# Attention and two mixture layers on one core: token pairs of 256, 512 and 320 columns in place of 256, 384 and 448

## The chip, the cores and the metric

The program runs on one core of one Trainium2 chip. The metric is the device time of one execution in microseconds (us); lower is better. The engines are named as in the profile: PE is TensorE (PEld its weight loads), DVE is VectorE, ACT is ScalarE, POOL is GpSimd, SP is the SyncE queue that issues every DMA.

## What is computed

Four batches of local attention with global tokens (8 heads, 512 local and 32 global tokens, head size 64), then two dense layers with gating over the resulting 2176 rows of 512 values. All matrices are float32.

```python
# attention: each local row sees itself +-32 neighbours and the 32 global keys; global rows see all keys
a_l   = sm(concat([s_lg, where(|i-j| <= 32, s_ll, -1e9)], axis=-1))
out_l = a_l @ concat([v_g, v_l]);   out_g = sm(s_g) @ concat([v_g, v_l])
# first and second product: gate, then 2048 -> 512
h = x @ w_in                                   # 512 -> 2048
x = (h * clip(h + 3, 0, 6) / 6) @ w_out        # 2048 -> 512
# third and fourth product: maximum of three, then 768 -> 512
h = max(max(x @ w1, x @ w2), x @ w3)           # 512 -> 768
out = h @ w_out2                               # 768 -> 512
```

## The kernel before, in words

The kernel is one list of steps. Each step is put on an engine with a due time and an estimated duration, and a planner (`Plan.order`) sorts all of them into one fixed order per engine. `STEPS` gives the spacing of the due times of the head pairs, for each batch; `TS`, `BIAS` and `SHARE` say which sums may go to DVE or to POOL and how the planner weighs the two. Each engine then runs its instructions strictly in that order and waits only on semaphores.

A float32 matrix product is made of three float32r matmuls (high by high, high by low, low by high), so every operand is split into a high and a low part: a copy on ACT (or DVE) and a subtraction on DVE (or POOL).

**Attention** (function `pair`, L364 to L482). Sixteen head pairs, four per batch. Each one runs scores on PE (L392), row maximum on DVE (L403), exponential on ACT (L409), normalisation on POOL (L431), transposes on PE (L443), a copy out of PSUM on ACT or DVE (L362), the product with the values on PE (L462), and the split of the result into the row buffer x on ACT and DVE (L478, L480). After every second pair the 32 global rows of both follow (`globals_`: L496, L522, L537 on PE).

**First product** (function `first`, L583). The rows lie in five chunks of x (`CHUNKS`); chunk c can be used when the attention over its rows is done. Three token pairs are formed: pair A are the two halves of chunk 0, pair B are chunks 1 and 2, pair C chunks 3 and 4. The two members of a pair and the two halves of the 2048 hidden columns make the four blocks of a seven-product scheme (products P1 to P7, additions in place of the eighth). So for each of eight groups g of hidden columns and each pair, four blocks of 12 matmuls run (two for A, which has both members in one chunk), each block goes through `relu` on ACT (L605) and `gate` on DVE (L607) into a buffer Q of seven slots, four subtractions make the sums (L611, run at L579), and the seven slots are stored to DRAM in two DMAs (L614): slots 0 to 2, then 3 to 6. For A and B the sums run on POOL, for C on DVE or POOL.

A's blocks run during the attention of batches 0 and 1, when the weights `w_in` are also decoded from their 64-bit form (`decode`, L544: ACT, three steps on DVE, one on POOL). B's blocks are asked for after batch 2 is issued, group by group: chunk 1, chunk 2, sums. C follows when attention has ended and its PSUM banks and buffers are handed on (`end_of_attention`).

**Second product** (`long_`, L736). Seven products over the groups, for each of the three pairs: a DMA loads a slot pair (L753), it is split (L688 on ACT, L579 on DVE or POOL), and 48 matmuls (L764) of 256 (A), 384 (B) or 448 (C) columns run. **Third product** (`quad`, L870): nine rounds of seven products of 6 matmuls (L885) for each pair, again of 256, 384 or 448 columns. **Fourth product** (L1006): 306 matmuls of 512 columns, in the order of the table `LAST`.

The columns of a pair are half of its rows: 256 + 384 + 448 = 1088 = 2176 / 2.

Of the kernel before, what the change touches and what calls it, by code (L numbers as in the profile page):

```python
# [242 lines left out]
def body(ctx, tc, q_n, k_n, v_r, msk, msk_g, w_in, w_o, w_3, w_4, out):  # L243
# [40 lines left out]
    fw = region("fw", 12544, F32, fw_es)
    re = region("re", 12544, F32R)
    rx = region("rx", 13824, F32R, p1, side="right")
    rq = region("rq", 5376, F32, p1, side="right")
    rr = region("rr", 11328, F32R, side="right")
# [294 lines left out]
    def first(p, g, due):  # L583

        n = TOK[p][1]
        Q = Buf(T["q" + p])
# [26 lines left out]
        for i, k in ((0, 3), (3, 4)):  # L613
            op("SP", 0.5, lambda i=i, k=k: nc.sync.dma_start(  # L614
                out=gs[p][:, g, i:i + k], in_=q(i, k).rearrange("p (s n) -> p s n", s=k)), due + 8,
               r=[(Q, i + j) for j in range(k)], w=[(gk, (p, g, i))], kb=k * n / 2, what="gstore")
        return due

# [473 lines left out]
```

## Time and profile before

| | |
|---|---|
| median of 3 runs | 767.35 us (766.35 to 767.74) |
| the profiled execution's own time | 766.48 us |
| its span in the profile | 764.7 us |
| PE busy | 742.8 us (97%), 5114 matmuls |
| DVE, ACT, POOL busy | 521.5 (68%), 396.8 (52%), 175.6 us (23%) |
| matmuls of the first product (L597) | 960 |
| matmuls of the second (L764) and third product (L885) | 1008 and 1134 by the program |
| granted TensorE clock | 1.00 (2.4 GHz) in stretches of 20 us, but for 40 to 60 us (0.91) |

The span is what the profiler saw from the first to the last instruction; 1.8 us of the execution's time lie around it. The page gives for each engine the time in which an instruction was under way. Matmuls overlap one another, so a busy PE says only that something was in flight. A pace is read from the starts: the start of the first matmul after a run, less the start of the run, divided by the matmuls between them.

### The profile page before, as it was taken

The page shows a single profiled execution, that of the slowest core. Times are in us where ns is not written, and L with a number is a line of the kernel's source. Part 1 is how long each engine was busy: PE and PEld are TensorE (multiplying, and loading weights), DVE is VectorE, ACT ScalarE, POOL GpSimd, SP SyncE. Part 2 cuts the span into 40 slices and gives each one's busy share as a digit, 9 for nine tenths or more (in the row PEclk, how much of TensorE's full clock was granted, in tenths as well). Part 3 has the DMA queues.
Part 4 walks back from the last instruction along what each step waited for, and adds up shares of the span by engine and source line. Part 5 has one row for each costly group of instructions (what it writes and reads, how often), then busy time and mean ns, then how long its engine had stood idle before and what let it go on. Part 6 is the DMA issues. An engine that isn't in the chain of part 4 may idle for free.

```text
span 764.7 us, 13733 instructions
## 1 busy us (share of the span) xinstructions
PE 742.8 (97%) x5114; PEld 669.3 (88%) x5114; DVE 521.5 (68%) x1081; ACT 396.8 (52%) x877; POOL 175.6 (23%) x182
## 2 busy tenths in 40 slices
PE   7889999899999999999999999999999999999997
PEld 4667777688999989999999999998999999998886
DVE  4889975555444687469987688988877787576100
ACT  6966777775643343346655557664344233245221
POOL 3658795254526210000100000020000010010000
PEclk9999999999999999999999999999999999999999
DMA  8257764335137666588657687501244462149312
GB/s 286 66 172 261 252 214 161 100 130 181 76 116 258 233 243 227 217 266 267 189 152 233 187 270 214 172 28 28 85 143 137 127 233 84 56 129 317 112 56 69
DMA packets 63234, 128.94 MB, mean 169 GB/s; under 512 B 5184, under 2 KB 40512, under 8 KB 63168
## 3 DMA queue, kind: packets, MB, share of 16 engines
q1 hardware_dynamic: 63168, 128.07, 50.7%
q8 instruction: 40, 0.66, 0.4%
q14 instruction: 26, 0.21, 0.1%
HBM read 84.14 MB, written 43.91 MB: 167 GB/s over the span
## 4 chain that ended last, share of the span: by engine, by line
PE 80%; DVE 7%; ACT 4%; DMA 3%; POOL 3%; issue 2%; SPq 0%; DVEq 0%; POOLq 0%; ACTq 0%
PE bank L885 21%; PE bank L597 21%; PE bank L764 19%; PE bank L1006 9%; PE o L462 3%; PE s L443 2%; ACT tbuf L409 2%; PE s L392 2%; POOL rq L579 1%; PE o L537 1%; DMA fw<-gsB 1%; POOL tbuf L431 1%; DVE rq L559 1%; PE s L496 1%; DMA vr<-in_v_dram 1%
## 5 line engine op out<-in xcount | busy, mean ns | idle before, releaser
L597 PE MATMUL bank<-rx,rw 128*128 128x384 f32 (+2 forms) x960 | 196.3, 361 | 0.3 <-DVE rq L607 0.3
L597 PEld LDWEIGHTS bank<-rx,rw 128*128 128x128 f32 x960 | 172.9, 188 | 18.6 <-issue 4.3
L764 PE MATMUL bank<-rr,rw 128*128 128x448 f32 (+2 forms) x912 | 157.6, 333 | 0.3 <-DVE rr L579 0.2
L764 PEld LDWEIGHTS bank<-rr,rw 128*128 128x128 f32 x912 | 150.2, 189 | 7.2 <-DVE rr L579 1.0
L688 ACT CAST rr<-fw 128x768 fp32r<-128x768 f32 (+2 forms) x76 | 62.2, 819 | 55.0 <-PE bank L764 36.8
L579 DVE TENSOR_TENSOR rr<-fw,rr 128x768 fp32r<-128x768 f32 (+2 forms) x75 | 72.8, 974 | 22.7 <-ACT rr L688 21.9
L885 PE MATMUL bank<-rw,rr 128*128 128x384 f32 (+1 forms) x474 | 81.0, 317 | 0.4 <-DVE rw L579 0.4
L885 PEld LDWEIGHTS bank<-rw,rr 128*128 128x128 f32 x474 | 75.3, 189 | 1.7 <-DVE rw L579 0.8
L579 POOL TENSOR_TENSOR rq<-rq 128x256 f32<-128x256 f32 (+1 forms) x64 | 62.7, 990 | 52.5 <-DVE rq L607 51.1
L431 POOL TENSOR_TENSOR tbuf<-tbuf,nm 128x448 f32<-128x448 f32 x64 | 62.8, 1002 | 48.5 <-DVE nm L422 34.3
L885 PE MATMUL bank<-re,rr 128*128 128x448 f32 x306 | 67.1, 368 | 0.0
L409 ACT ACTIVATE tbuf<-tbuf,nm 128x224 f32<-128x224 f32 x128 | 60.3, 473 | 11.9 <-DVE nm L403 11.9
L885 PEld LDWEIGHTS bank<-re,rr 128*128 128x128 f32 x306 | 56.8, 188 | 4.9
L362 ACT COPY rf<-bank 128x448 f32<-128x448 f32 (+2 forms) x74 | 33.9, 463 | 52.1 <-PE bank L885 44.6
L607 DVE SCALAR_TENSOR_TENSOR rq<-rq,bank 128x384 f32<-128x384 f32 (+2 forms) x56 | 33.5, 599 | 37.9 <-ACT rq L605 37.8
L605 ACT ACTIVATE rq<-bank,three 128x384 f32<-128x384 f32 (+2 forms) x56 | 34.6, 618 | 44.7 <-PE bank L597 43.0
L969 DVE TENSOR_TENSOR rf<-rf,bank 128x384 f32<-128x384 f32 (+2 forms) x72 | 37.6, 530 | 19.3 <-PE bank L885 18.3
L403 DVE CUSTOM_DVE_ANT_0 tbuf<-s,mask 128x224 f32<-128x224 f32 x128 | 42.8, 383 | 8.5 <-PE s L392 8.5
L579 POOL TENSOR_TENSOR rf<-rf 128x256 f32<-128x256 f32 (+1 forms) x10 | 8.9, 892 | 170.6 <-DVE rf L674 71.5
L462 PE MATMUL o<-pt,vr 128*64 128x128 f32 (+1 forms) x512 | 35.5, 280 | 7.2 <-ACT rw L570 3.1
L462 PEld LDWEIGHTS o<-pt,vr 128*64 128x64 f32 (+1 forms) x512 | 29.0, 138 | 15.3 <-issue 5.6
L392 PE MATMUL s<-kr,qr 64*64 64x224 f32 x512 | 33.1, 379 | 6.3 <-DMA kr<-in_kn_dram 5.3
(106 smaller groups left out, 1065.7 us busy)
## 6 DMA issues: line engine op xcount, KB each, us to landing
fw<-gsC SPq DMA_DIRECT2D x28, 448.0 KB, 4.2
raw<-in_w_dram SPq DMA_DIRECT2D x24, 512.0 KB, 4.2
fw<-gsB SPq DMA_DIRECT2D x28, 384.0 KB, 4.1
raw<-in_w_in_dram SPq DMA_DIRECT2D x16, 512.0 KB, 4.3
raw<-in_w_o_dram SPq DMA_DIRECT2D x16, 512.0 KB, 4.2
fw<-gsA SPq DMA_DIRECT2D x28, 256.0 KB, 3.3
gsB<-rq SPq DMA_DIRECT2D x8, 768.0 KB, 3.8
gsC<-fw SPq DMA_DIRECT2D x6, 896.0 KB, 4.0
```

What stands on the lines that cost most here:

```text
L392: nc.tensor.matmul(SB[u][hh]()[m:m + 64, v * WIN:v * WIN + WIN], lhsT=Q()[o:o + 64, 128 * i + m:128 * i + m + 64], rhs=K()[o:o + 64, 128 * ...
L403: nc.vector.tensor_tensor_reduce(out=tb[hh]()[:, v, 0:WIN], in0=sb[hh]()[:, v * WIN:v * WIN + WIN], in1=mask()[:, i], scale=-0.125, scalar ...
L409: nc.scalar.activation(out=t, in_=t, func=ACTF.Exp, scale=-1.0, bias=nm()[:, 0, hh, v:v + 1], accum_out=nm()[:, 1, hh, v:v + 1])
L431: nc.gpsimd.tensor_tensor(out=t, in0=t, in1=r, op=ALU.mult)
L462: nc.tensor.matmul(ob()[64 * hh:64 * hh + 64, 128 * i:128 * i + 128], lhsT=V()[0:n, hh, i + kb], rhs=PT[u][hh]()[0:n, at:at + 128], start= ...
L579: ENG[e].tensor_tensor(out=out, in0=a, in1=b, op=f)
L597: nc.tensor.matmul(ps()[:, 0:m], lhsT=w[:, i, k], rhs=xs(c)[:, j, k], start=(k == 0 and s == 0), stop=(k == KC - 1 and s == 2))
L688: op("ACT", act(n) + 0.01, lambda: nc.scalar.copy(out=out(0), in_=src()), due, r=r, w=[(w, "hi")], what=what + "_hi")
L764: nc.tensor.matmul(A[e]()[:, 0:n], lhsT=w[:, 2 * fp + f, u, e], rhs=r[:, v, f], start=(seed is None and fp + f + s == 0), stop=(fp == 3 an ...
L885: nc.tensor.matmul(bank()[:, 0:n], lhsT=w[:, u, k], rhs=r[:, v, k], start=(start and k + s == 0), stop=(k == 1 and s == 2), skip_group_che ...
L969: op("DVE", dve(n), lambda q=q, src=src, mv=mv: nc.vector.tensor_tensor(out=mv(q)(), in0=mv(q)(), in1=src(), op=ALU.max), -200, r=[bank], ...
L1006: nc.tensor.matmul(A(), lhsT=H2[h]()[:, 384 * p + i * 128:384 * p + (i + 1) * 128], rhs=cols(w4[h], l, 1, 512), start=(h == 0 and s == 0), ...
```

## The change

The chunks become 512, 512, 512, 320 and 320 rows, so that chunks 1 and 2 are exactly batches 1 and 2. Pair B has 512 columns, pair C 320, A stays at 256. The Q buffers have four slots in place of seven and three places instead of two: slots 0 to 2 are stored first, the four sums then overwrite slots 0 to 3, and these are stored in a second DMA. So the sums have to wait until the first store has been read out. B's sums may now go to DVE or POOL, like C's. B's groups 0 to 2 are issued together, then 3 and 4: first chunk 1 for all groups of the set, then chunk 2. Groups 5 to 7 of B come after attention, ahead of C, and C's blocks may use all eight PSUM banks. The spacing of batch 1's head pairs goes from 12 to 16, `BIAS` from -1 to -0.5 and `SHARE` from 0.5 to 0. The last piece of the second product and the rounds of the third take the pairs in the order C, A, B, and the fourth product begins with C's rows. Buffers move to other places in their regions, and `w_4` is decoded in three rounds instead of one.

```diff
-CHUNKS = [(0, 512), (512, 384), (896, 384), (1280, 448), (1728, 448)]
-TOK = {"A": (0, 256), "B": (512, 384), "C": (1280, 448)}
+CHUNKS = [(0, 512), (512, 512), (1024, 512), (1536, 320), (1856, 320)]
+TOK = {"A": (0, 256), "B": (512, 512), "C": (1536, 320)}
...
-LAST = [(512, 384), (896, 384), (1280, 384), (1664, 256), (1920, 256), (0, 256), (256, 256)]
+LAST = [(1536, 384), (1920, 256), (0, 256), (256, 256), (512, 384), (896, 384), (1280, 256)]
...
-TS = "C"
-STEPS = (8, 12, 12, 16)
+TS = "BC"
+STEPS = (8, 16, 12, 16)
 LAG = 84.0
-BIAS = -1.0
-SHARE = 0.5
+BIAS = -0.5
+SHARE = 0.0
...
-    T["qA"] = Spot(1792, places(rq, 0, 1792, 2))
-    T["qB"] = Spot(2688, places(rq, 0, 2688, 2))
-    T["qC"] = Spot(3136, [((fw, 9408), (fw, 6144), (rq, 0))[int(i)] for i in "01201021"])
+    T["qA"] = Spot(1024, places(rq, 0, 1024, 3))
+    T["qB"] = Spot(2048, [(rq, 2048 * (i % 3)) for i in range(5)] + [(fw, 8704), (fw, 10752), (rq, 4096)])
+    T["qC"] = Spot(1280, [(fw, 6144), (fw, 7424)] + [(rq, 1280 * (i % 3)) for i in range(NG - 3)] + [(fw, 6144)])
...
-    def first(p, g, due):
+    def first(p, gs_, due):
...
-            for a in range(2):
-                ps, x, f, i = Buf(T["l"]), X[c], g + NG * a, 2 - 2 * a + h
+            for g, a in ((g, a) for g in gs_ for a in range(2)):
+                ps, f, i, k = Buf(T["bank" if p == "C" else "l"]), g + NG * a, 2 - 2 * a + h, m // n
...
-        for o, a, b in ((4, 3, 2), (6, 1, 3), (5, 1, 4), (3, 0, 5)):
-            op(DP if p in TS else "POOL", dp(n) if p in TS else pool(n), lambda e="POOL", o=o, a=a, b=b: tt(
-                e, q(o), q(a), q(b), ALU.subtract), due, r=[(Q, a), (Q, b)], w=[(Q, o)], what="tsum", two=True)
...
+        for g in gs_:
+            store(p, g, Q[g], 0, 3, due)
+            for a, b, o in ((3, 2, 2), (1, 3, 3), (1, 2, 1), (0, 1, 0)):
+                op(DP if p in TS else "POOL", dp(n) if p in TS else pool(n), lambda e="POOL", g=g, o=o, a=a, b=b: tt(
+                    e, q(g, o), q(g, a), q(g, b), ALU.subtract), due, r=[(Q[g], a), (Q[g], b)], w=[(Q[g], o)], what="tsum",
+                   two=True)
+            store(p, g, Q[g], 3, 4, due)
...
-            for g in range(NG):
+            for g in ([0, 1, 2], [3, 4]) if b else [[g] for g in range(NG)]:
                 due1 = first("AB"[b // 2], g, due1)
...
-    for g in range(NG):
-        due1 = first("C", g, due1)
+    for p, g in [("B", g) for g in range(5, NG)] + [("C", g) for g in range(NG)]:
+        due1 = first(p, [g], due1)
...
-    ORDER = [(i, c) for i, c in zip((0, 1, 0, 0, 1, 1), "BBCACA")] + [(i, c) for i in range(2, 9) for c in "BCA"]
+    ORDER = [(i, c) for i, c in zip((0, 1, 0, 1, 0, 1), "CCAABB")] + [(i, c) for i in range(2, 9) for c in "CAB"]
```

Two places show how the instructions move. The first is PE in batch 2's attention: the stretch from the fourth group of global rows (L537) to the fifth. L392 are scores, L443 and L522 transposes, L462 products with values, L597 blocks of the first product; xN counts matmuls in a row (the trace lists scores and products with values at twice this count). Before:

```order
L392 MATMUL s<-kr,qr 64x224 x8
L597 MATMUL bank_100<-rx,rw 128x384 x12
L462 MATMUL o<-pt,vr 64x128 x16
L392 MATMUL s<-kr,qr 64x224 x24
L443 MATMUL s<-ident,tbuf_107 128x128 x4
L443 MATMUL s<-ident,tbuf_109 128x128 x4
L443 MATMUL s<-ident,tbuf_111 128x128 x4
L443 MATMUL s<-ident,tbuf_113 128x128 x4
L522 MATMUL s<-ident,tg 128x128 x5
L462 MATMUL o<-pt,vr 64x128 x16
```

With the change, in the same stretch:

```order
L392 MATMUL s<-kr,qr 64x224 x16
L597 MATMUL bank_99<-rx,rw 128x512 x12
L462 MATMUL o<-pt,vr 64x128 x16
L392 MATMUL s<-kr,qr 64x224 x16
L597 MATMUL bank_100<-rx,rw 128x512 x12
L443 MATMUL s<-ident,tbuf_107 128x128 x4
L443 MATMUL s<-ident,tbuf_109 128x128 x4
L443 MATMUL s<-ident,tbuf_111 128x128 x4
L443 MATMUL s<-ident,tbuf_113 128x128 x4
L522 MATMUL s<-ident,tg 128x128 x5
L597 MATMUL bank_99<-rx,rw 128x512 x12
L462 MATMUL o<-pt,vr 64x128 x16
```

One block of 384 columns stands there before, three of 512 now. The stretch ahead of it holds two of A's and one of B's before, one of A's and two of B's now; the whole attention holds 16 blocks of A and 17 of B's 32 before, and 16 of A and 18 of B's 32 now.

The second place is POOL in batch 1, from the first of A's sums. L579 rq<-rq are A's sums, L571 the last step of a weight's decoding, L431 the normalisation of a head pair. Before:

```order
L571 TENSOR_TENSOR rw<-rq,rw 128x512
L579 TENSOR_TENSOR rq<-rq 128x256 x4
L571 TENSOR_TENSOR rw<-rq,rw 128x512 x2
L579 TENSOR_TENSOR rq<-rq 128x256 x4
L571 TENSOR_TENSOR rw<-rq,rw 128x512
L431 TENSOR_TENSOR tbuf_115<-tbuf_115,nm 128x2x224
L431 TENSOR_TENSOR tbuf_117<-tbuf_117,nm 128x2x224
L579 TENSOR_TENSOR rq<-rq 128x256
L431 TENSOR_TENSOR tbuf_119<-tbuf_119,nm 128x2x224
L431 TENSOR_TENSOR tbuf_121<-tbuf_121,nm 128x2x224
L571 TENSOR_TENSOR rw<-rq,rw 128x512 x2
```

With the change:

```order
L571 TENSOR_TENSOR rw<-rq,rw 128x512 x3
L579 TENSOR_TENSOR rq<-rq 128x256 x4
L571 TENSOR_TENSOR rw<-rq,rw 128x512 x2
L431 TENSOR_TENSOR tbuf_115<-tbuf_115,nm 128x2x224
L431 TENSOR_TENSOR tbuf_117<-tbuf_117,nm 128x2x224
L571 TENSOR_TENSOR rw<-rq,rw 128x512
L579 TENSOR_TENSOR rq<-rq 128x256 x4
L431 TENSOR_TENSOR tbuf_119<-tbuf_119,nm 128x2x224
L431 TENSOR_TENSOR tbuf_121<-tbuf_121,nm 128x2x224
L579 TENSOR_TENSOR rq<-rq 128x256 x4
L571 TENSOR_TENSOR rw<-rq,rw 128x512 x2
```

Before, the first set of sums follows five weight steps, and from the third on sets are broken up by other work; now seven weight steps come first, and each set of four stands in one piece. After A's last sums POOL has 28 normalisations in a row now; before, B's 32 sums of 384 columns stood among and behind these. The change has B's sums on DVE.

## Rows read from the trace of the kernel before

**Rows 1.** The page, part 1: busy time and share of the span.

```profile
PE 742.8 (97%) x5114; PEld 669.3 (88%) x5114; DVE 521.5 (68%) x1081; ACT 396.8 (52%) x877; POOL 175.6 (23%) x182
```

**Rows 2.** Busy time by stretch: start:end, length, then PE, PEld, DVE, ACT, POOL (instructions).

```profile
35.00:112.00 77.00, 71.82 (x594) 55.06 (x592) 69.93 (x154) 55.06 (x144) 60.98 (x56) 0.98 0.67 222
...
134.00:154.00 20.00, 17.72 (x225) 13.55 (x225) 11.40 (x51) 15.49 (x54) 5.47 (x6) 1.00 0.29 95
...
221.00:333.00 112.00, 111.67 (x585) 105.09 (x582) 71.87 (x124) 43.13 (x74) 21.88 (x18) 1.00 0.65 230
333.00:492.00 159.00, 158.67 (x936) 151.90 (x936) 131.08 (x179) 93.12 (x134) 9.46 (x6) 1.00 0.71 219
492.00:691.00 199.00, 197.80 (x1195) 189.97 (x1194) 157.08 (x276) 81.79 (x153) 15.16 (x15) 1.00 0.33 107
```

**Rows 3.** Timeline of PE, the starts of global rows: start us, duration us, instructions.

```profile
35.09 1.36 PE L537 MATMUL o<-pt,vr 128*64 128x32 f32 x40
...
111.70 1.31 PE L537 MATMUL o<-pt,vr 128*64 128x32 f32 x40
...
134.16 1.36 PE L537 MATMUL o<-pt,vr 128*64 128x32 f32 x40 [0.20 <-DVE rx L480]
...
154.24 1.36 PE L537 MATMUL o<-pt,vr 128*64 128x32 f32 x40 [0.20 <-DVE nm L422]
...
179.51 1.36 PE L537 MATMUL o<-pt,vr 128*64 128x32 f32 x40
```

**Rows 4.** Timeline of PE around 180 us, where it has no gap.

```profile
175.70 1.98 PE L462 MATMUL o<-pt,vr 128*64 128x128 f32 x32
177.61 1.97 PE L443 MATMUL s<-ident,tbuf 128*128 128x128 f32 x16
...
180.70 1.22 PE L496 MATMUL s<-kr,qr 128*64 128x304 f32 x8
181.85 2.35 PE L597 MATMUL bank<-rx,rw 128*128 128x384 f32 x12
184.14 1.74 PE L392 MATMUL s<-kr,qr 64*64 64x224 f32 x32
185.81 1.98 PE L462 MATMUL o<-pt,vr 128*64 128x128 f32 x32
```

**Rows 5.** Timeline of PE: first, third and fourth product without a gap.

```profile
277.67 48.91 PE L597 MATMUL bank<-rx,rw 128*128 128x448 f32 x240 [0.33 <-DVE rq L607]
...
584.72 2.25 PE L885 MATMUL bank<-rw,rr 128*128 128x384 f32 x12
...
602.81 1.60 PE L885 MATMUL bank<-rw,rr 128*128 128x256 f32 x12
604.24 1.60 PE L885 MATMUL bank<-rr 128*128 128x256 f32 x12
...
626.64 1.21 PE L885 MATMUL bank<-rw,rr 128*128 128x384 f32 x6
...
628.40 5.37 PE L885 MATMUL bank<-rw,rr 128*128 128x384 f32 x30
633.60 2.63 PE L885 MATMUL bank<-re,rr 128*128 128x448 f32 x12
...
714.42 23.28 PE L1006 MATMUL bank<-rw,re 128*128 128x512 f32 x102
737.54 2.88 PE L1006 MATMUL bank<-rw 128*128 128x512 f32 x12
```

**Rows 6.** Sums on POOL (page, part 5) and on DVE (timeline).

```profile
L579 POOL TENSOR_TENSOR rq<-rq 128x256 f32<-128x256 f32 (+1 forms) x64 | 62.7, 990 | 52.5 <-DVE rq L607 51.1
...
351.82 1.29 DVE L579 TENSOR_TENSOR rf<-fw 128x512 f32<-128x512 f32 x2
```

**Rows 7.** Stores of the first product (page's DMA view): size, median us to landing.

```profile
gsA<-rq SPq DMA_DIRECT2D x8, 384.0 KB, 4.4
...
gsB<-rq SPq DMA_DIRECT2D x8, 768.0 KB, 3.8
```

More of the change, by code (lines that the diff above doesn't have):

```diff
@@ L280, in region @@
         return r
-    rw = region("rw", 16384, F32R)
+    rw = region("rw", 16640, F32R)
     fw_es, p1 = ExitStack(), ExitStack()
[L284 to L288, printed above, removed]
+    fw = region("fw", 12800, F32, fw_es)
+    re = region("re", 12800, F32R)
+    rx = region("rx", 13312, F32R, p1, side="right")
+    rq = region("rq", 6144, F32, p1, side="right")
+    rr = region("rr", 10752, F32R, side="right")
     rf = region("rf", 10752, F32, side="right")
@@ L340, in body @@
     T["g1"] = tag("g1", 2, [128, 4], F32, "att")
-    for c, at in enumerate((0, 4096, 7168, 10240, 0)):
+    for c, at in enumerate((0, 5120, 9216, 0, 2560)):
         T["x", c] = Spot(8 * CHUNKS[c][1], [(rx, at)])
@@ L598, in mm @@
                                              stop=(k == KC - 1 and s == 2))
-                op("PE", mmt(12, m), mm, 1e4 + due, r=[wi[f], x], w=[ps], what="first")
+                op("PE", mmt(12, m), mm, 1e4 + due, r=[wi[f], X[c]], w=[ps], what="first")
                 due += 3
-                out = lambda i=i, m=m: q(i, m // n)
-                z = [(Q, i + k) for k in range(m // n)]
+                out = lambda g=g, i=i, k=k: q(g, i, k)
+                z = [(Q[g], i + j) for j in range(k)]
                 us = 0.2 + m * .00098
@@ L609, in first, with store @@
                    what="gate")
-        for o, a, b in ((4, 3, 2), (6, 1, 3), (5, 1, 4), (3, 0, 5)):
-            op(DP if p in TS else "POOL", dp(n) if p in TS else pool(n), lambda e="POOL", o=o, a=a, b=b: tt(
-                e, q(o), q(a), q(b), ALU.subtract), due, r=[(Q, a), (Q, b)], w=[(Q, o)], what="tsum", two=True)
[L613 to L616, printed above, removed]
-        return due
+        for g in gs_:
[5 more added lines that the diff above has]
+            store(p, g, Q[g], 3, 4, due)
+        return due
+    def store(p, g, Q, at, k, due):
+        n = TOK[p][1]
+        op("SP", 0.5, lambda: nc.sync.dma_start(
+            out=gs[p][:, g, at:at + k], in_=Q()[:, 0:k * n].rearrange("p (s n) -> p s n", s=k)), due + 8,
+           r=[(Q, j) for j in range(k)], w=[(gk, (p, g, at))], kb=k * n / 2, what="gstore")
     s = 6
@@ L695, in body @@
     hk = Buf()
-    YAT, WS, LU = dict(B=0, C=3072, A=6656), 8704, 5376
+    YAT, WS, LU = dict(C=0, A=2560, B=4608), 8704, 6144
     for p in "ABC":
@@ L699, in body @@
     T["wb"] = Spot(2048, places(fw, 0, 2048, 4) + [(rf, WS)])
-    T["lp"] = Spot(4096, [(rw, at) for at in (0, 4096, 12288, 0, 4096, 0, 12288)])
-    T["grA"], T["g2A"] = Spot(512, places(fw, 9408, 512, 4)), Spot(1024, places(rw, 8192, 1024, 4))
-    T["gr"], T["g2"] = Spot(896, [(fw, at) for at in (9408, 10304, 11200, 8512)]), Spot(1792, places(rr, 0, 1792, 3))
+    T["lp"] = Spot(4096, [(rw, at) for at in (0, 4096, 12544, 0, 4096, 0, 12544)])
+    T["grA"], T["g2A"] = Spot(512, places(fw, 8704, 512, 8)), Spot(1024, places(rw, 8192, 1024, 4))
+    T["gr"], T["g2"] = Spot(1024, places(fw, 8704, 1024, 4)), Spot(2048, places(rr, 0, 2048, 3))
     WO = {}
@@ L788, in body @@
     turns = [(p, c, None) for p, c in zip(("P1", "P2", "P1", "P1", "P2", "P2", "P5", "P5", "P5"), "AABCBCBCA")]
-    turns += [(p, c, {"P6": 0}.get(p, True)) for p in ("P6", "P7", "P4") for c in "ABC"] + [("P3", c, None) for c in "BCA"]
+    turns += [(p, c, {"P6": 0}.get(p, True)) for p in ("P6", "P7", "P4") for c in "ABC"] + [("P3", c, None) for c in "CAB"]
     plan.event(lambda: (p1.close(), rr.open(), rf.open()), ("lp", "rx", "rq"), ("rr", "rf"))
@@ L851, in body @@
     top = 0
-    for p in "BCA":
+    for p in "CAB":
         n = TOK[p][1]
@@ L946, in body @@
             L3[i] = units(w_blocks(w_3, i, t, 18), t - 6)
-            for k in range(3) if i == 5 else ():
+            for k in (i - 4,) if 4 <= i < 7 else ():
                 W = Buf(T["wd"])
```

32 lines of the change are left out of this document (16 added, 16 removed).

## Prediction

> **What bounds the kernel now.** I read the page's first part, the busy time by stretch, and then PE's timeline. PE is busy for 742.8 us, 97% of the span [rows 1]; the next engine, DVE, for 68%. From 221 us on PE lacks 0.3 us in 112, 0.3 in 159 and 1.2 in 199 [rows 2], so from there the time is the number of matmuls by their pace, and nothing else. The reader should see that "busy" hides something before that. From 134 to 154 us PE is busy for 17.7 of 20 us, with no other engine near its limit (DVE 11.4, POOL 5.5, ACT 15.5) [rows 2].
>
> So I price what PE must do in a stretch of attention by its pace where nothing holds it up, and look at the rest. Starts that follow one another [rows 3, 4]: scores 185.81 - 184.14 = 1.67 us, transposes 179.51 - 177.61 = 1.90, products with values 177.61 - 175.70 = 1.91, so 5.48 for a head pair. Every second pair adds global rows, 180.70 - 179.51 = 1.19, their scores 181.85 - 180.70 = 1.15, and five transposes, 5 x 1.90/16 = 0.59. Two pairs cost 2 x 5.48 + 2.93 = 13.9 us. A block of the first product is 12 matmuls. The paces are [rows 5]: 256 columns (604.24 - 602.81)/12 = 119.2 ns, 384 columns 5.20/30 = 173.3 ns, 512 columns 23.12/102 = 226.7 ns, so 2.08 us for a block of 384 and 2.72 for one of 512.
>
> From one group of global rows to the next [rows 3] PE does two head pairs and the blocks that the order puts there:
> - 35.09 to 111.70 (four pairs, 14 blocks of A): 76.6 us, work 27.8 + 38.1, rest 10.7. Here DVE is busy for 69.9 of 77 us and POOL for 61.0 [rows 2]: the decoding of the weights holds PE up.
> - 111.70 to 134.16 (two blocks of A, one of B): 22.5, work 21.4, rest 1.0.
> - 134.16 to 154.24 (one block of B): 20.1, work 16.0, **rest 4.1**.
> - 154.24 to 179.51 (five blocks of B): 25.3, work 24.3, rest 1.0.
>
> With enough blocks at hand PE loses 1 us per stretch; in the third it has one block. The code says why: B's blocks take two PSUM banks in turn, in the order in which they were made, so behind the two chunk-1 blocks of group 0 stands a chunk-2 block, which has to wait for batch 2.
>
> **The change, part by part, on the profiled execution's 766.48 us** (the median of the runs, 767.35, is 0.87 higher).
>
> *Blocks in batch 2's attention.* Three groups now start with chunk 1, so six blocks need nothing of batch 2. The order puts three of 512 columns into the stretch of the 4.1 us. PE's work there becomes 13.9 + 3 x 2.72 = 22.1 us, more than the 20.1 that the stretch took, so PE should be its limit again, with the rest of 1.0 of its neighbours: -3.1 us. These blocks are missing from the time after attention, so this is a gain and no shift. Bounds: 0, if the stretch just grows by the new blocks; -4.1, if nothing is left. Ahead of it A's blocks move a little later within batches 0 and 1; I leave the rest of 10.7 as it is, since the decoding on DVE, which it waits for, is unchanged. Its bounds belong to the rivals.
>
> *Widths.* The counts of matmuls stay; 384 and 448 columns become 512 and 320. In the third product two rounds take 626.64 - 584.72 = 41.92 us for 84 matmuls of each of the three widths, 499.0 ns for one of each [rows 5]. Less 119.2 and 173.3 that leaves 206.5 for 448 columns, while the line through 384 and 512 has 200.0 there: 448 carries 6.5 ns that the others don't. For 320 there is no row. The line through 256 and 384 gives 146.3; with the same extra it is 152.8; nothing tells which, so I take the middle, 149.5. One of each then costs 119.2 + 226.7 + 149.5 = 495.4, 3.6 less. By the program there are 378 of each in the third product (-1.4) and 336 in the second (-1.2). In the first, 448 runs at 48.91/240 = 203.8 [rows 5], so a 384 and a 448 cost 377.1 and the new two 376.2: 384 times 0.9 is -0.3. Sum -2.9, bounds -6.5 and +0.7 (1098 times 3.25 either way).
> Against this stands a rule: the Trainium skill (TensorE: Matmul & The Clock Gate, Back-to-back issue gap) has a matmul's spacing at full clock as N/2.4 + 2.5 ns, a straight line, by which any split of 1088 columns over as many matmuls costs the same. Our 256, 384 and 512 do lie on a line, with some 13 ns in place of 2.5, but 448 lies above it [rows 5]. By the rule this term is 0 and the sum 763.4.
>
> *Sums in place.* B's 32 sums leave POOL (a sum there takes 0.99 us on the mean of A's and B's [rows 6]) and go to DVE, at 0.65 each [rows 6], 21 us in all: some 13 of them in attention, where DVE has room after 112 us (11.4 of 20), some 8 after it. There the stage gets shorter, from 15 blocks of 2.08 and 32 of 2.45 to 14 of 2.72 and 32 of 1.79, 109.5 to 95.5 us, so DVE goes from 71.9 of 112 [rows 2] to at most 80 of 96: cover enough, at nothing. What is new is that the first sum of a group waits for the first store. B's store of 768 KB, so far the second one, takes 3.8 us to land and A's of 384 KB 4.4 [rows 7]. Queued behind such a wait on DVE are gates, which hold the two banks, and row maxima; on POOL weight steps and normalisations, for which PE waits. The order puts other work between, and a third buffer gives the room, so I put it at 0; the far end is the third rival.
>
> *Entrances of the second and third product.* A's and B's loads can go earlier, and the third product starts with C, whose operands are the narrowest and are ready first; B's, the widest, come last. DVE runs at 131 of 159 us and 157 of 199 [rows 2], so it has no more than a fifth to spare. PE lost 1.5 us over both products, so there is at most 1 to gain, and with DVE late by a few operands, some 4 x 1.0 us, 4 to lose. Taken as 0. The SP queue carries the same bytes; a store that waits holds up the loads behind it, but the loads of the weights lead by more than one.
>
> Sum: -3.1 - 2.9 = -6.0, so 760.5 in the profiled execution and **761.4 us** in the median.
>
> **Rivals.**
> 1. *Attention before 112 us shortens too*: half of its rest of 10.7 us goes, because POOL is freer. 761.4 - 5.3 = 756.1. For it: A's buffers are three now. Against it: DVE at 91% there, with work that stays.
> 2. *The new blocks only stretch batch 2.* If the chain of row maximum, exponential and normalisation sets the pace of a pair, not PE, the stretch grows by what is put in. ACT is at 15.5 of 20 there and gets two more relus. The 3.1 are lost: 764.5. Against it: the next stretch, with five blocks, lost 1.0.
> 3. *POOL waits for A's stores (the slower case).* In batches 0 and 1 POOL is busy for 61.0 of 77 us [rows 2], so it has 16.0 idle, 2.0 for each of A's eight groups. A wait of 4.4 us that is quite uncovered would ask for 35; from 2.0 us per group on, each further us costs 8, since weight steps and normalisations queue behind it. At 3.2 us a group: 8 x 1.2 = 9.6, 771.0. For it: POOL's queue is strict and the sets of sums stand whole. Against it: they come after more weight steps than before.
> 4. *320 is as dear as 448*: 152.8 in place of 149.5 makes the width term +0.7, so 765.0. The rule above, with a term of 0, gives 764.3 in the median and is counted here.
>
> **How the numbers follow.** Chances: forecast 0.42, rival 1 0.15, rival 2 0.14, rival 3 0.17, rival 4 0.12. A measurement here can tell 0.2%, 1.5 us: below 765.8 is faster, above 768.9 slower. Forecast and rival 1 are faster; of rivals 2 and 4, just under the edge, I count half as no change, since 1 us at an entrance takes them there. Faster 0.70, same 0.13, slower 0.17. The range goes from 754.0 (rival 1 with part of the width's lower bound) to 771.0 (rival 3 as priced), which leaves out the dearer half of rival 3 and the tail of rival 1.
>
> **What would show it.** Right: between the fourth and fifth L537 some 23 us with three blocks; 320 columns at 146 to 153 ns; A's sums not waiting long for a store on POOL; no gap of PE over 1 us after attention. Wrong: a POOL that sits idle for a gsA store in batches 0 and 1, the third L537 group later than 112 us by more than the moved blocks, or PE gaps where the second product begins.

## The result, and the profile after

| | before | after |
|---|---|---|
| median of 6 runs on one chip | 766.47 us (766.07 to 767.74) | 758.78 us (757.97 to 760.2) |
| ratio after to before, 95% interval | | 0.9899 [0.9885, 0.9913] |
| profiled execution, span | 766.48, 764.7 us | 757.97, 755.9 us |

The change makes the kernel 1.0% faster, 7.7 us in the medians and 8.8 in the spans, which the stages below add up to; 761.4 was forecast, 754.0 to 771.0 the range. The page of the kernel after, part 1, answers to [rows 1]:

```profile
PE 734.9 (97%) x5114; PEld 636.6 (84%) x5114; DVE 524.9 (69%) x1090; ACT 394.7 (52%) x864; POOL 161.3 (21%) x170
```

PE has the same 5114 matmuls and is busy for 7.9 us less. The busy time by stretch answers to [rows 2] (start:end, length, then PE, PEld, DVE, ACT, POOL, granted clock, DMA share, GB/s):

```profile
35.00:117.00 82.00, 73.95 (x624) 55.56 (x622) 69.87 (x162) 56.85 (x151) 60.42 (x59) 1.00 0.65 215
139.00:161.00 22.00, 21.88 (x246) 17.66 (x243) 11.77 (x50) 16.61 (x52) 7.29 (x8) 1.00 0.28 86
161.00:232.00 71.00, 71.00 (x710) 56.96 (x707) 40.08 (x132) 41.53 (x123) 15.33 (x16) 1.00 0.35 128
232.00:327.00 95.00, 95.00 (x565) 88.36 (x561) 72.00 (x130) 38.80 (x70) 16.97 (x13) 1.00 0.75 271
327.00:482.00 155.00, 154.74 (x955) 142.61 (x954) 128.99 (x187) 89.40 (x130) 4.97 (x3) 1.00 0.69 213
482.00:682.00 200.00, 199.21 (x1190) 181.30 (x1189) 154.28 (x267) 86.34 (x158) 27.10 (x27) 1.00 0.36 113
```

From 139 us on PE has hardly a gap; in the stretch where it was busy for 17.72 of 20 us it now is for 21.88 of 22. What is left is in the first line: 8 us without a matmul in batches 0 and 1. The starts of the global rows and of the products, on PE's timeline [rows 3, 5] (the lines of the second, third and fourth product stand six further down in this kernel: L770, L891 and L1012):

```profile
34.76 1.36 PE L537 MATMUL o<-pt,vr 128*64 128x32 f32 x40
...
116.50 1.31 PE L537 MATMUL o<-pt,vr 128*64 128x32 f32 x40
138.84 1.31 PE L537 MATMUL o<-pt,vr 128*64 128x32 f32 x40
161.52 1.31 PE L537 MATMUL o<-pt,vr 128*64 128x32 f32 x40
189.99 1.36 PE L537 MATMUL o<-pt,vr 128*64 128x32 f32 x40
...
232.21 94.71 PE L597 MATMUL bank<-rx,rw 128*128 128x512 f32 x552
326.76 11.68 PE L770 MATMUL bank<-rw 128*128 128x256 f32 x96
...
600.08 3.68 PE L891 MATMUL bank<-rw 128*128 128x320 f32 x24
603.59 1.60 PE L891 MATMUL bank<-rr,rw 128*128 128x256 f32 x12
...
620.86 3.38 PE L891 MATMUL bank<-rw,rr 128*128 128x320 f32 x22
...
682.50 3.79 PE L1012 MATMUL bank<-rw 128*128 128x512 f32 x16
```

Read with the prediction's prices (13.9 us for two head pairs, 2.72 for a block of 512 columns; the rest is what a stretch takes beyond them), the stages are:

- Batches 0 and 1, up to the third L537: 15 blocks of A by 116.50 us, against 14 by 111.70. With a block's 2.72 added, before would be at 114.42: **2.1 us worse**. The rest of the stretch is 81.7 - 27.8 - 40.8 = 13.1 us, against 10.7.
- From there to the second product: 326.76 - 116.50 = 210.3 us. In the kernel before, 12 matmuls of the second product ran early, for 1.43 us, and the remainder began at 332.71; so its second product counts from 331.28. That gives 219.6, less the one block of 2.72 that it had still to do: 216.9. **6.6 us better**. Of this, 1.6 are width: 384 pairs of a 384 and a 448 cost 377.1 ns each, of a 512 and a 320 now 226.7 + 146.3. The other **5.0** are filling: the stretch from the fourth L537 to the fifth went from a rest of 4.1 to 22.7 - 13.9 - 3 x 2.72 = 0.6, the rest of the one ahead of it shrank by 0.7 and that of the one from the sixth to the seventh by 0.4, and 0.4 stays unassigned. The one behind it, with five blocks, has the rest of 1.0 that it had.
- Second and third product: 682.50 - 326.76 = 355.7, against 691.27 - 331.28 = 360.0: **4.3 us better**. 24 matmuls of 320 columns take 3.51 us, **146.3 ns** each; a round of the third product takes 20.78 us for 42 of each width, 494.8 ns for one of each, against 499.0 before. 714 times 4.2 is 3.0. Of the other 1.2, gaps make 0.5: PE was idle for 1.5 us in these two products before [rows 2] and has gaps of 0.26 and 0.79 now. The remaining 0.7 stay unassigned.

Sum: 2.1 - 6.6 - 4.3 = -8.8.

### The profile page after: what moved, and what is told of

Same layout as the page of the kernel before. It is cut to its first block, busy times and chain, and to the rows that moved or that the text cites. A ratio compares the mean times of both kernels' runs of the same rounds, so it can differ in the third digit from the quotient of the medians.

```text
span 755.9 us, 13671 instructions
## 1 busy us (share of the span) xinstructions
PE 734.9 (97%) x5114; PEld 636.6 (84%) x5114; DVE 524.9 (69%) x1090; ACT 394.7 (52%) x864; POOL 161.3 (21%) x170
## 4 chain that ended last, share of the span: by engine, by line
PE 82%; DMA 5%; DVE 4%; POOL 4%; ACT 3%; issue 1%; SPq 0%; POOLq 0%; ACTq 0%; DVEq 0%
PE bank L891 25%; PE bank L770 21%; PE bank L597 19%; PE bank L1012 9%; PE o L462 3%; POOL rq L579 2%; PE s L443 2%; PE s L392 2%; ACT tbuf L409 2%; DMA raw<-in_w_in_dram 1%; DMA vr<-in_v_dram 1%; DVE rq L559 1%; PE o L537 1%; POOL tbuf L431 1%; DVE rq L562 1%
## 5 line engine op out<-in xcount | busy, mean ns | idle before, releaser
L597 PE MATMUL bank<-rx,rw 128*128 128x512 f32 (+1 forms) x960 | 196.2, 361 | 1.8 <-DVE rq L607 1.5
L597 PEld LDWEIGHTS bank<-rx,rw 128*128 128x128 f32 x960 | 162.2, 188 | 29.1 <-issue 4.7
L770 PE MATMUL bank<-rr,rw 128*128 128x320 f32 (+2 forms) x912 | 155.6, 332 | 0.3 <-DVE rr L579 0.3
L770 PEld LDWEIGHTS bank<-rr,rw 128*128 128x128 f32 x912 | 141.0, 189 | 14.2 <-DVE rr L579 1.1
L694 ACT CAST rr<-fw 128x1024 fp32r<-128x1024 f32 (+2 forms) x76 | 62.2, 820 | 55.0 <-PE bank L770 40.6
L579 DVE TENSOR_TENSOR rr<-fw,rr 128x1024 fp32r<-128x1024 f32 (+2 forms) x76 | 70.4, 935 | 19.5 <-ACT rr L694 18.7
L431 POOL TENSOR_TENSOR tbuf<-tbuf,nm 128x448 f32<-128x448 f32 x64 | 62.4, 997 | 82.4 <-DVE nm L422 65.2
L579 POOL TENSOR_TENSOR rf<-rf 128x256 f32<-128x256 f32 (+1 forms) x18 | 14.4, 810 | 227.4 <-DVE rf L579 109.2
L605 ACT ACTIVATE rq<-bank,three 128x512 f32<-128x512 f32 (+1 forms) x60 | 37.8, 631 | 45.8 <-PE bank L597 43.1
L607 DVE SCALAR_TENSOR_TENSOR rq<-rq,bank 128x512 f32<-128x512 f32 (+1 forms) x60 | 36.9, 618 | 35.6 <-ACT rq L605 35.2
L891 PE MATMUL bank<-rw,rr 128*128 128x320 f32 (+1 forms) x270 | 49.0, 328 | 0.8 <-DVE bank L900 0.8
L975 DVE TENSOR_TENSOR rf<-rf,bank 128x320 f32<-128x320 f32 (+2 forms) x72 | 37.5, 530 | 17.6 <-PE bank L891 16.5
L891 PEld LDWEIGHTS bank<-rw,rr 128*128 128x128 f32 x270 | 42.8, 188 | 4.3 <-DVE bank L900 1.2
L462 PEld LDWEIGHTS o<-pt,vr 128*64 128x64 f32 (+1 forms) x512 | 27.9, 136 | 13.2 <-issue 3.6
L891 PE MATMUL bank<-rw 128*128 128x320 f32 (+1 forms) x216 | 38.8, 327 | 0.0
L462 PE MATMUL o<-pt,vr 128*64 128x128 f32 (+1 forms) x512 | 33.2, 276 | 5.7 <-DMA vr<-in_v_dram 1.9
L443 PE MATMUL s<-ident,tbuf 128*128 128x128 f32 x256 | 34.5, 278 | 3.8 <-POOL tbuf L431 2.7
L392 PE MATMUL s<-kr,qr 64*64 64x224 f32 x512 | 32.1, 373 | 4.9 <-DMA kr<-in_kn_dram 4.8
```

Of the source, the lines that this page charges most:

```text
L392: nc.tensor.matmul(SB[u][hh]()[m:m + 64, v * WIN:v * WIN + WIN], lhsT=Q()[o:o + 64, 128 * i + m:128 * i + m + 64], rhs=K()[o:o + 64, 128 * ...
L431: nc.gpsimd.tensor_tensor(out=t, in0=t, in1=r, op=ALU.mult)
L443: nc.tensor.transpose(FB[u][hh]()[:, at:at + 128], TB[u][hh]()[:, v, kb * 128:kb * 128 + 128], ident)
L462: nc.tensor.matmul(ob()[64 * hh:64 * hh + 64, 128 * i:128 * i + 128], lhsT=V()[0:n, hh, i + kb], rhs=PT[u][hh]()[0:n, at:at + 128], start= ...
L579: ENG[e].tensor_tensor(out=out, in0=a, in1=b, op=f)
L597: nc.tensor.matmul(ps()[:, 0:m], lhsT=w[:, i, k], rhs=xs(c)[:, j, k], start=(k == 0 and s == 0), stop=(k == KC - 1 and s == 2))
```

## The experiments

The planner makes one order out of the whole list, so every edit moves other steps too. The totals therefore mix effects: of the eleven whole kernels below, only e5, e10 and e11 came out within the time that the leading theory named. So each run is read by stage, from the profiled execution, and there is one of these for each kernel. "Blocks" are those done by the third L537; "2nd + 3rd" is the time from the second product's start to the fourth's. The kernel before ran beside them, with medians of 766.67 (e2 to e4), 766.68 (e5 to e8) and 767.45 us (e9 to e12).

| kernel | first L537 | third L537 (blocks) | 2nd product | 2nd + 3rd | median of runs | ratio to before |
|---|---|---|---|---|---|---|
| before | 35.09 | 111.70 (14) | 331.28 | 360.0 | 766.47 | |
| after | 34.76 | 116.50 (15) | 326.76 | 355.7 | 758.78 | 0.9899 |
| e5 after again | 34.71 | 115.58 (15) | 326.36 | 356.9 | 759.46 | 0.9914 [0.9896, 0.9932] |
| e2 groups one by one | 35.61 | 117.47 (15) | 333.50 | 362.3 | 770.38 | 1.0051 [1.0036, 1.0065] |
| e9 e2, weights earlier | 34.98 | 116.71 (15) | 330.05 | 355.4 | 760.78 | 0.9915 [0.9898, 0.9931] |
| e3 old widths | 36.35 | 117.91 (15) | 337.68 | 358.2 | 769.94 | 1.0041 [1.0026, 1.0057] |
| e4 due times 12 | 35.84 | 111.03 (14) | 330.15 | 361.7 | 766.56 | 0.9996 [0.9987, 1.0006] |
| e10 e4, weights earlier | 35.41 | 111.80 (14) | 330.46 | 355.6 | 762.21 | 0.9936 [0.9915, 0.9957] |
| e6 A's sums apart | 34.72 | 115.88 (15) | 325.21 | 363.2 | 763.66 | 0.996 [0.9948, 0.9972] |
| e7 B's sums on POOL | 36.44 | 119.71 (15) | 329.92 | 362.1 | 765.83 | 0.9991 [0.9977, 1.0004] |
| e8 due times 10 | 39.35 | 115.62 (14) | 330.25 | 355.1 | 760.47 | 0.9923 [0.9907, 0.9939] |
| e11 after, weights earlier | 36.26 | 117.21 (15) | 327.11 | 354.7 | 757.59 | 0.9875 [0.9856, 0.9894] |
| e12 due times 14 | 36.53 | 117.67 (15) | 329.28 | 355.8 | 760.62 | 0.99 [0.9877, 0.9923] |

**e1: the widths by themselves.** Nothing of the computation is left; 96 matmuls of each width run back to back, with the weight loads between.

```diff
+RUNS = ((512, 512), (256, 256), (320, 320), (384, 384), (416, 416), (448, 448), (480, 480), (512, 512), (448, 512), (448, 448))
...
+    for run, (n, step) in enumerate(RUNS):
+        for g in range(16):
+            bank = banks[g % 2]
+            for i, (u, v) in enumerate(((0, 0), (0, 1), (1, 0), (2, 2), (2, 3), (3, 2))):
+                nc.tensor.matmul(bank[:, 0:n], lhsT=r[:, 2048 + 128 * u:2048 + 128 * u + 128], rhs=r[:, step * v:step * v + n],
+                                 start=(i == 0), stop=(i == 5))
```

> Leaves out the whole computation: it only runs 96 matmuls back to back of each of the widths 512, 256, 320, 384, 416, 448, 480, 512 and 448 (rows 512 apart), 448 columns. If a width of 448 is dear by itself (the width theory), its starts are 203 to 207 ns apart here too, where the line through 384 and 512 has 200, and 320 is at 146. If the extra comes from the other engines' traffic in the kernel (rival), 448 is at 200 here. If it hangs on where the parts of the moving operand lie, the 448 with rows 512 apart differs from the 448 with rows 448 apart.

Rows of PE's timeline in e1, each from a window within one width (start, duration, matmuls). The pace is the duration less one matmul's (309, 368, 379 and 365 ns), over the count less one.

```profile
49.76 8.52 PE L30 MATMUL bank<-r 128*128 128x320 f32 x57
...
97.82 16.49 PE L30 MATMUL bank<-r 128*128 128x448 f32 x79
...
117.70 16.63 PE L30 MATMUL bank<-r 128*128 128x480 f32 x76
...
179.71 15.56 PE L30 MATMUL bank<-r 128*128 128x448 f32 x76
```

320 columns: (8.52 - 0.31)/56 = 146.6 ns. 448: 206.7 in its first run, 202.6 in its last, with the same addresses, and 202.7 with operands 512 apart. In the same way 256, 384 and 512 give 120.0, 173.4 and 226.7, 416 gives 188.9 and 480 gives 216.7. Against N/2.4 ns, the number of columns over the full clock of 2.4 GHz, 256, 320, 384 and 512 lie 13.3 to 13.4 ns higher, and 416, 448 and 480 lie 15.6 to 20.0 higher. No other engine was at work, so the dearness of 448 is no matter of their traffic; the addresses do not explain it either, and why 448 has two values stays open.

**e2 and e9: B's groups one by one.** e9 also decodes the third product's weights 24 ahead in the plan, in place of 18.

```diff
-            for g in ([0, 1, 2], [3, 4]) if b else [[g] for g in range(NG)]:
+            for g in [[g] for g in range(5)] if b else [[g] for g in range(NG)]:
...
-            L3[i] = units(w_blocks(w_3, i, t, 18), t - 6)
+            L3[i] = units(w_blocks(w_3, i, t, 24), t - 6)
```

> The changed kernel with B's groups issued one by one again, chunk 1 and chunk 2 in turn; widths and sums in place stay. Filling theory (blocks that need only batch 1 fill batch 2's attention): the order has no block left in the stretch between the fourth and fifth L537, which then takes some 20 us for 13.9 us of work, a rest of 6 instead of 0.6, and five blocks more come after attention: 4 to 6 us slower than the change, 763 to 765. Rival (the gain is the widths and the later stages alone): within 1 us of the change, 758 to 760.

> B's groups one by one as in the run e2, and besides the third product's weights decoded 24 us ahead in the plan instead of 18, which leaves the order up to the attention's end as it was in e2. In e2 the second product began 6.7 us later than in the changed kernel, and second and third product together took 6.6 us more, with PE waiting 1.4, 0.8 and 1.6 us for operands where the third one begins. Theory (the filling of batch 2 is worth what the start of the second product shows, and the rest of e2's loss is an accident of the order on DVE and ACT at the third product's entrance): second product again at 332 to 334, PE's waits at the third product's entrance under 1 us in sum, second and third product 355.5 to 358, time 763.5 to 767. Rival (one by one also costs something in the later products): waits and 362 us stay, time 769 to 771.

In both, the stretch between the fourth and the fifth L537 holds no block at all: it takes 17.2 and 17.4 us for 13.9 of work, a rest of 3.3 and 3.5, close to the 4.1 of before. That shows what filled it. From the third L537 to the second product e9 needs 213.3 us, against 210.3, 210.8 and 209.9 in after, e5 and e11: **3.0 us** for the three-group start. The cleanest pair is e9 and e11, which differ by this edit alone: 3.4 us in this stage and 3.2 in the medians (760.78 and 757.59). e2 needs 216.0, and its total of 770.38 is far above the 763 to 765 expected. Up to the second product e2 and e9 have the same order on every engine, so e2's other 2.7 us are no matter of the order. PE's waits show them, first in e2:

```profile
162.69 2.60 PE L462 MATMUL o<-pt,vr 128*64 128x128 f32 x32 [2.06 <-DMA vr<-in_v_dram]
...
512.84 0.38 PE L891 MATMUL bank<-rr 128*128 128x256 f32 x1 [1.41 <-ACT rr L828]
514.00 0.85 PE L891 MATMUL bank<-rr 128*128 128x256 f32 x5 [0.78 <-DVE rr L579]
516.48 1.86 PE L891 MATMUL bank<-rr 128*128 128x256 f32 x7 [1.63 <-ACT rf L362]
```

and in e9, at the place of the first of these rows:

```profile
160.87 1.98 PE L462 MATMUL o<-pt,vr 128*64 128x128 f32 x32 [0.66 <-DMA vr<-in_v_dram]
```

The first wait is for a load of vr, the values of a head pair, and it was 1.4 us longer in e2. The other three stand where the third product begins. The windows of e2 around them (PE busy, then the granted clock) show a second price:

```profile
160.00:164.00 4.00, 1.94 (x38) 0.99 0.85 303
164.00:168.00 4.00, 4.00 (x47) 0.59 0.01 5
168.00:172.00 4.00, 4.00 (x18) 1.00 0.01 2
...
512.00:516.00 4.00, 1.24 (x6) 0.93 0.00 0
516.00:520.00 4.00, 3.52 (x14) 0.50 0.00 0
520.00:524.00 4.00, 4.00 (x17) 0.71 0.00 0
524.00:528.00 4.00, 4.00 (x24) 1.00 0.00 0
```

After the wait of 2.06 us PE ran at 0.59 of full speed on the mean of the next 4 us, that is mostly at the lower of its two levels, 1.2 GHz; after the three waits it had 0.50 and 0.71. The 3.8 us of waiting and, as an estimate, 4 x (0.50 + 0.29) = 3.2 us of lost clock cover the 6.6 us by which e2's second and third product are longer than after's. In e9 the weights are decoded earlier, the three waits are gone, and the two products take 355.4 us, as in after. So that part of e9's theory holds. The other part took e2's late start of the second product for the worth of the filling, and misses: in e9 it starts at 330.05 us, not at 332 to 334, and the time of 760.78 is below the 763.5 to 767 named, since the late vr did not return.

**e3: the old widths in the new scheme** (chunks and columns of before; buffers, tables and places fitted).

```diff
-CHUNKS = [(0, 512), (512, 512), (1024, 512), (1536, 320), (1856, 320)]
-TOK = {"A": (0, 256), "B": (512, 512), "C": (1536, 320)}
+CHUNKS = [(0, 512), (512, 384), (896, 384), (1280, 448), (1728, 448)]
+TOK = {"A": (0, 256), "B": (512, 384), "C": (1280, 448)}
```

> The changed kernel with the chunks and pairs of before (256, 384, 448 columns) and the buffers moved to hold them; groups, sums in place, due times and the order C, A, B stay. Width theory: second and third product lose 4.2 ns for each of 714 triples of matmuls, 3.0 us, and the first product 1.6, less what the narrower blocks fill better or worse: 762 to 765. Rival (width is worth nothing, the filling is all): 757 to 760.

A round of the third product takes 684.08 - 663.12 = 20.96 us on its timeline, 499.0 ns for one of each again (last two rows):

```profile
225.76 2.38 PE L462 MATMUL o<-pt,vr 128*64 128x128 f32 x32 [1.94 <-ACT tg L508]
...
663.12 3.04 PE L891 MATMUL bank<-rr,rw 128*128 128x256 f32 x24
...
684.08 3.04 PE L891 MATMUL bank<-rr 128*128 128x256 f32 x24
```

Second and third product are 2.5 us longer than after's, near the 3.0 of the pace. From the third L537 to the second product e3 needs 9.5 us more than after; 1.6 of them are pace, the rest comes with another order in batches 2 and 3, with the wait of 1.94 us in the first row and a granted clock of 0.97 from 161 to 232 us. That part is not told apart further, and because of it e3's time of 769.94 misses the 762 to 765 expected.

**e4, e10, e8 and e12: the due times.** Four kernels set other spacings for the head pairs of batches 0 and 1; e10 is e4 with the weights 24 ahead.

```diff
-STEPS = (8, 16, 12, 16)
+STEPS = (8, 12, 12, 16)      # e4, e10
+STEPS = (10, 16, 12, 16)     # e8
+STEPS = (8, 14, 12, 16)      # e12
```

> The changed kernel with the spacing of batch 1's head pairs back at 12. The order then puts six blocks of A ahead of the second L537 and eight between it and the third, in place of four and eleven. If the later start of A's blocks is what made batches 0 and 1 lose 13.1 us instead of 10.7 (spacing theory), this is faster by up to 2.4 us, 756 to 758. If that loss comes from the sums in place (rival) or from decoding alone, and the wider spacing pays, it is 758.5 to 762.

> The due times of batch 1's head pairs 12 apart as in the run e4, and the third product's weights 24 us ahead. In e4 batches 0 and 1 had 3.8 us less of rest than the changed kernel, PE then waited 3.3 us for a vr in batch 2, and second and third product took 6.0 us more, of which 2.2 were waits at the third product's entrance. Theory (each order stands and falls with its entrance): waits there under 1 us, second and third product 355.5 to 358, time 761 to 763, still not better than the changed kernel, since the vr wait remains. Rival (DVE is short there whatever the order, and 16 apart was lucky): 766 as before.

> Due times only: a head pair of batch 0 is set at 10 apart instead of 8. By the order, batches 0 and 1 then have 5 and 9 blocks between their L537 groups, as the kernel before had, and batch 2 has 4 and 3 and 5. Theory (batches 0 and 1 are set by the decoding on DVE, and what they lost against before came from blocks put later): the rest goes from 13.1 back to about 10.7, time 2 us below the changed kernel, 756 to 757, if the third product is entered without a gap. Rival (the 2.4 us came from in-place sums or from chance): the rest stays at 13 and the time at 758 to 760. Second rival (another order costs at the entrance of the third product, as in the earlier variants): the start of the second product is earlier, but 2 to 6 us are lost behind it.

> The changed kernel with batch 1's head pairs due 14 apart instead of 16; blocks between the L537 groups are the same, 4, 11, 3, 3, 5, 6, 2. A try at a version better than both. Theory (in batches 0 and 1 DVE sets the pace, and due times only decide which weight step comes first): rest there 11 to 13 us, 757 to 760. Rival (16 put A's blocks off, which the run with 12 bears out by a rest of 9.3): rest 9 to 11, 755 to 757.

With 12, the third L537 stands at 111.03 and 111.80 with 14 blocks, so at 113.8 and 114.5 with a 15th: the 2.1 us that after lost there are back (before: 114.4, after and e5: 116.5 and 115.6). So 16 in place of 12 costs them. The traces of all kernels bear it out, by the order of A's blocks. With four of them ahead of the second L537 and eleven behind it, as in after, the rest of batches 0 and 1 is 12.3 to 14.7 us in nine traces; with six and eight (e4, e10) it is 9.3 and 10.5, with five and nine (before, e8) 10.7 and 10.4. The clock is not the reason: from 35 to 60 us 0.93 of it was granted in before, e4 and e10, and 1.00 in after and e5, which are the slower ones there. But with 12 PE then waits for a vr that SP issues only at 164.28 us, behind three other loads, here on PE's timeline of e4:

```profile
169.99 2.92 PE L462 MATMUL o<-pt,vr 128*64 128x128 f32 x32 [3.28 <-DMA vr<-in_v_dram]
```

And of e10:

```profile
170.29 3.34 PE L462 MATMUL o<-pt,vr 128*64 128x128 f32 x32 [2.81 <-DMA vr<-in_v_dram]
```

In e4 the clock is 0.72 in the 4 us from 172 on, and the second product begins 3.4 us later than after's. So 16 is the better choice on the whole: it loses 2 us early and saves more in batch 2. e11 and e10, which differ by these due times alone, are 4.6 us apart (757.59 and 762.21). e4's time of 766.56 is above both ranges named for it, since it also lost 6.0 us in the second and third product. e10 repeats the test of the entrance: the 2.2 us of waits that e4 had there shrink to 0.6, second and third product go from 361.7 to 355.6 us, and the time falls in the 761 to 763 that was expected. e8 misses: the rest of batches 0 and 1 does fall, to 76.3 - 27.8 - 14 x 2.72 = 10.4 us, but the stretch begins 4.6 us later, and the time, 760.47, is not the 756 to 757 expected. A rest counted from a moved start is no gain. In e12 the blocks stay at four and eleven and the rest is 12.5, as the theory had it; its time is 0.6 us above the range named.

**e6 and e7: the sums.** e6 gives A's sums slots of their own (seven slots in two places, both stores behind the sums); in it the fifth and sixth of A's stored operands stand in each other's place, with the same work. e7 lets B's sums run on POOL.

```diff
-    T["qA"] = Spot(1024, places(rq, 0, 1024, 3))
+    T["qA"] = Spot(1792, places(rq, 0, 1792, 2))
...
+            sums = ((3, 2, 4), (1, 3, 6), (1, 4, 5), (0, 5, 3)) if p == "A" else ((3, 2, 2), (1, 3, 3), (1, 2, 1), (0, 1, 0))
```

```diff
-TS = "BC"
+TS = "C"
```

> A's sums go to slots of their own again (seven slots in two buffers instead of four in three), so that none waits for a store; B and C stay in place. Blocks between the L537 groups stay 4, 11 for batches 0 and 1. Theory (in place costs nothing on the path): POOL's 4.1 us of waiting for gsA go, but the rest of batches 0 and 1 stays within 1.5 us of the changed kernel's, since DVE's decoding sets it; time within 2 us of the changed kernel. Rival (the stores' wait on POOL is what made batches 0 and 1 worse by 2.4): the rest falls from 13.1 to 10.7 or below and the time to about 756. Second rival (two buffers are too few): ACT or DVE evictions wait for a free buffer, batches 0 and 1 longer by over 2 us.

> B's 32 sums go back from DVE to POOL, still in place; everything else as in the changed kernel. Theory (DVE has room for them): nothing gained on DVE's side; DVE's busy time falls by about 21 us, the time stays within 2 us of the changed kernel, and POOL is seen waiting for gsB, 768 KB each, without PE losing more than 1 us for it. Rival (DVE's 13 us in attention cost PE something): batches 2 and 3 lose less than the 1.6 us of rest that they have, so faster by at most 1.6. Second rival (POOL's strict queue): weight steps and normalisations wait behind B's sums, batches 2 and 3 longer by 2 us or more.

POOL's waits in batches 0 and 1 of after (in all, times, longest; us):

```profile
POOL rw L571 <- ACT rw L570: 8.1, 5, 2.6
POOL rw L571 <- DVE rq L557: 5.9, 1, 5.9
POOL rq L579 <- DMA gsA<-rq: 4.1, 3, 3.7
```

In e6 the last of these rows is gone, and the rest of batches 0 and 1 is 81.2 - 68.6 = 12.6 us, between the 13.1 and 12.3 of after and e5. So no cost of the stores' wait shows beyond this scatter of 0.8, and it does not explain the 2.1 us. In e7 POOL waits far longer between 117 and 330 us, now for B's stores:

```profile
POOL rq L579 <- DMA gsB<-rq: 21.1, 3, 10.6
```

PE's waits in the same stretch of e7 are this one row, and POOL is not in it:

```profile
PE o L462 <- DMA vr<-in_v_dram: 0.8, 2, 0.5
```

From the third L537 to the second product e7 takes 210.2 us, as after does (210.3): no cost to PE shows with B's sums on either engine. The totals of e6 and e7, 4.2 and 6.4 us above e5's, are off for another reason. Both have the three waits at the third product's entrance that e2 has, to the digit (1.6, 1.4 and 0.8 us), and e7 is behind by 3.2 us already at the third L537, half of it by its start.

The traces show a mark of the orders that lose there. Four sums of weights for the third product (L579, rf<-rf of 256 columns) stand close together in after, three of them in this row of DVE and the fourth on POOL at 471.47 us:

```profile
470.24 1.09 DVE L579 TENSOR_TENSOR rf<-rf 128x256 f32<-128x256 f32 x3
```

In e2 they are spread over 25 us:

```profile
472.98 0.74 POOL L579 TENSOR_TENSOR rf<-rf 128x256 f32<-128x256 f32 x1 [101.58 <-DVE rf L680]
481.44 0.75 POOL L579 TENSOR_TENSOR rf<-rf 128x256 f32<-128x256 f32 x1 [7.71 <-DVE rf L680]
...
496.75 0.42 DVE L579 TENSOR_TENSOR rf<-rf 128x256 f32<-128x256 f32 x1
497.95 0.43 DVE L579 TENSOR_TENSOR rf<-rf 128x256 f32<-128x256 f32 x1
```

They are spread like this in e4, e6 and e7 too, and in no other kernel: there, before included, they lie within 7 us. That this delay makes the operands late is likely, but no run changes it alone.

**e5 and e11: the change again, and with the weights earlier.**

> The changed kernel itself once more, as the yardstick of the three that run beside it on this chip: 758 to 760 us. Any theory expects the same; what it adds is a second trace of the same order of work, which tells how far the gaps of batches 0 and 1 (13.1 us of rest in the first trace, 10.7 before) and the gaps of PE at the third product's entrance (none) belong to the order and how far to one execution. If they belong to the order: rest 12 to 14, no gap of PE over 0.8 us after attention.

> The changed kernel with the third product's weights 24 us ahead instead of 18. There PE waited nowhere at the third product's entrance, so theory (nothing to gain where nothing waits): within 1.5 us of the changed kernel, 757.5 to 760.5. Rival (earlier decoding on DVE takes the second product's operands' place): PE waits for rr or rw in the second product, 1 to 3 us, 760 to 763.

e5 is within 0.7 us of the first measurement, with a rest of 12.3 us and two gaps of 0.8 us. The one of 0.79 us at the end of the third product is the same in both traces and belongs to the order; the other, of 0.76 at 455 us, is not in the first trace. e11 has the lowest time. Its interval lies below that of e5 but overlaps with that of the first measurement, and it has four executions, so a version that beats the change is not shown.

## Why the prediction was right, and where not

- **Blocks in batch 2's attention, -3.1: right.** The stretch became 22.7 us, with a rest of 0.6 instead of the 1.0 forecast. The comparison of traces gives 5.0 for all of the filling; e9, which takes back the three-group start, gives 3.0 to 3.4 for that. Where the other 1.6 to 2.0 come from was not tried. Rival 2 is out: the stretch took 22.7 us with its three blocks, where the old 20.1 and two blocks more would have made 25.5.
- **Widths, -2.9: mis-sized.** Measured are 4.2 ns x 714 = 3.0 in the second and third product and 1.6 in the first, together -4.6. The step that failed is "I take the middle" between 146.3 and 152.8 for 320 columns: 320 lies on the line of 256, 384 and 512 (146.3 in the kernel, 146.6 in e1), and of the kernel's widths only 448 lies above it. Rival 4 is out. (The 203.8 for 448 columns in the first product is a duration over a count; by starts, with PE's next row at 326.42 us, it is (326.42 - 277.67)/240 = 203.1, which makes 0.3 us over the 384.) The rule of the Trainium skill (TensorE: Matmul & The Clock Gate, Back-to-back issue gap), N/2.4 + 2.5 ns, by which the term is 0, is given there for a matmul by itself. It does not hold for this stream of matmuls with weight loads: the rows lie 13 ns above N/2.4 at the four good widths and up to 20 at 448.
- **Batches 0 and 1, "I leave the rest of 10.7 as it is": wrong by 2.1 us.** Rival 1, half of that rest gone, had the sign wrong. I looked at DVE's load, which is unchanged, and not at the due times of batch 1, which the diff sets from 12 to 16, nor at the blocks of A that they put later. e4 and e10 show that this is the cause.
- **Sums in place, 0: right.** POOL waited for A's stores 4.1 us in three waits, where rival 3 needed more than 2.0 in each of eight groups; e6 and e7 show no cost of it. DVE came to 72.0 of 95 us after attention, under the bound of 80 of 96.
- **Entrances, 0: right within 1.2 us (0.5 of gaps, 0.7 unassigned), but partly by luck: this was the least safe term.** I bounded it at 4 us of late operands. Four orders with small differences elsewhere (e2, e4, e6, e7) lost 6.0 to 7.4 us in the second and third product, most of it at the third one's entrance, as waits of PE of 2.2 to 3.8 us and as lower clock. In e9 and e10, with the third product's weights decoded earlier, the loss is gone; so the place of this work in the order is the cause, though which of its steps is not shown. The change's own order happens to have it early enough.
- **Not tried by themselves**: `BIAS`, `SHARE`, the eight banks for C, B's groups 5 to 7 ahead of C, and the order C, A, B. What each of them is worth stays open.

Two misses of opposite sign, -1.7 at the widths and +2.1 in batches 0 and 1, nearly cancelled. The whole came out lower because of filling beyond the one stretch (1.9) and the 1.2 us in the second and third product. That the sum was near is in part luck.

## What to carry over

When a planner reorders a whole program, read an experiment by stages: the start of each stage, like for like in work done, tells what an edit is worth, and the total may be off by 6 us through an accident elsewhere (6.6 in e2). Price a split of columns by the measured pace of each width: the line through 256 and 384 was right for 320 and is off by 2.6 to 6.7 ns for 448. To price an edit, compare two kernels that share everything else, such as e9 and e11. Where PE is the bound and runs without gaps, late operands can cost their wait and nearly as much again in clock (3.8 and an estimated 3.2 us in e2).

## What was not expected

- Waits of PE of 2.06 us (e2) and 3.28 us (e4) were followed by a granted clock of 0.59 (164 to 168 us) and of 0.72 (172 to 176 us). The same order with a wait of 0.66 us (e9) kept 1.00. But after waited 2.00 us at 50 us (for POOL's normalisation) and had 1.00 from 35 to 60 us, so a wait of this length does not always cost clock; what decides was not tried.
- The same order gives other clocks: e11 and after have one order on all engines until well into the second product, and yet e11's clock was 0.95 in the first 35 us, after's 1.00, and its first L537 came 1.5 us later.
- 448 columns took 202.6 and 206.7 ns a matmul within one run, on the same addresses.
